# Weight conversion in blocks of 512 words, first-batch softmax by row sums, and a new split of small work between ScalarE and VectorE

## The chip, the cores and the metric

The kernel runs on one core of one Trainium2 chip. The metric is the device time of one execution in microseconds; the kernel before was timed three times, with a median of 1607.3 us (1606.66 to 1612.92).

## What is computed

Pooled attention followed by two MLPs, on 2304 tokens. Queries are averaged in pairs, so 4 batches of 8 heads have 576 queries against 1152 keys of width 64. The cut reference:

```python
q_pool = q.reshape(B, H, S // 2, 2, D).mean(axis=3)
scores = (1 / sqrt(D)) * q_pool @ k.transpose(0, 1, 3, 2)
attn = exp(scores - max(scores)); attn = attn / (sum(attn) + 1e-9)
x = (attn @ v), heads side by side          # 2304 x 512
h = x @ moe_w_in;  x = maximum(0.01 * h, h) @ moe_w_out       # 512 -> 2048 -> 512
h = x @ moe2_w_in; x = where(h > 0, h, exp(min(h, 0)) - 1) @ moe2_w_out
```

The weights of the MLPs arrive as 64-bit floats, that is as pairs of 32-bit words, and are converted on the chip.

## The kernel before

**Units of work.** Attention goes by pairs of heads, 16 pairs in all, four for each batch. For one head the 576 queries are two halves of 288, and the 1152 keys are nine blocks of 128. `weigh` multiplies one key block with one half (two matmuls into an `e` bank of PSUM), and ScalarE takes the exponential into `pt`. `value` multiplies `pt` with the value block and sums the nine blocks of a half in the single `o` bank. Before that, `maxima` finds each query's largest score: PE fills an `s` bank with 384 scores and VectorE (DVE) reduces it. The queries' part with the largest score in it (`ql`) is transposed into `qB`, so that the maximum is subtracted by the matmul itself.

**Batch 0 differs** (`FULL = (0,)`). It multiplies the unrounded exponentials in full precision, a matmul that shows as two instructions in the trace. Its value tile carries columns of ones beside the 64 value columns, so the sums of the exponentials come out in the other half of the `o` bank. At the end of each half ScalarE copies the sums to `tm` (L573), DVE takes their reciprocal over 64 x 288 (L575) and multiplies (L577). Only then is `o` free for the next half. Batches 1 to 3 instead sum the exponentials in `pacc` on DVE, and once a pair `normalise` turns these into quotients: ten small matmuls against ones (L599), three small DVE operations, transposes through the single `t` bank, and a multiplication on DVE.

**Queries.** `q_split` adds the two queries of a pair on POOL (L428), scales on DVE (L430), rounds on DVE into `qh` (L432), and leaves the rest `ql` to POOL (L435).

**Weights.** Each MLP has 32 tiles of 128 x 512, converted once and kept in DRAM in two parts. `convert` works in blocks of `CW` = 256: a load into `cr` (a ring of two), two DVE operations on the high word (L292, L295), two on ScalarE (L298 scales the low word, L300 takes the size of the high one into a tile `cm`), an addition on POOL (L302) and a last DVE operation (L304). Then the tile is rounded on ScalarE (L325), the rest formed on POOL (L327), and `ws` (a ring of three) is stored. `CONV` spreads the 32 tiles of the first MLP over the attention of batch 0, those of the second over most of batch 1.

**MLPs.** `mlp` splits its input into a rounded part `xs` (on DVE, L262) and a rest, then runs three matmuls for each product (L714 up, L752 down). The first MLP of batch 0 begins when the attention of batch 0 is done.

**Order.** Every operation goes into `Program` with an engine, a cost and a rank; `schedule` replays these costs and fixes one order for each engine. On the chip each engine runs its instructions in that order, so an instruction that waits holds up all those behind it on its engine. Transfers go through SP's queue in the same manner.

## Time and profile before

| | us |
|---|---|
| median of three runs | 1607.3 |
| profiled execution | 1605.11 |
| its span, first to last instruction | 1603.3 |
| PE busy | 1461.6 |
| DVE busy | 1072.8 |
| ScalarE (ACT) busy | 885.6 |
| POOL busy | 565.9 |

Busy time counts an engine's instructions, not its waits. Pairs of heads begin their first `weigh` at 28, 93, 148, 211 (batch 0), 270, 374, 485 and 561 us (batch 1), which gives the stretches that are used below; the later pairs follow at 82 to 93 us each. All numbers of "the span" are microseconds from the first instruction. A group of a line gives count, busy time, mean of one in ns, then the idle time of the engine just before and what ended it.

### The profile page before, as it was taken

To read this page: it belongs to the slowest core of one execution; us is meant where nothing else is said; L and a number is where in the kernel's file an instruction comes from. 1 tells how busy PE (TensorE), PEld (TensorE's weight loads), DVE (VectorE), ACT (ScalarE), POOL (GpSimd) and SP (SyncE) were. 2 spreads that over 40 slices of the span, in tenths; PEclk is the share of its full clock that TensorE was granted. 3 is DMA by queue.
4 is the path that set the end of the run, shared out by engine and by line. 5 is a ranking of instruction groups with operands and counts; after the bars stand their busy time and mean duration, and the time that the engine had idled before them with its cause. 6 is when DMAs were issued, how large, how long until landed. Compare 5 with 4: busy or idle time off the path is not lost.

```text
span 1603.3 us, 28154 instructions
## 1 busy us (share of the span) xinstructions
PE 1461.6 (91%) x9884; PEld 1379.9 (86%) x9884; DVE 1072.8 (67%) x2461; ACT 885.6 (55%) x2429; POOL 565.9 (35%) x660
## 2 busy tenths in 40 slices
PE   5777887878988999999999999999999999799998
PEld 3566666877877999999999999899999999799898
DVE  6788788988989877766667667866767564123222
ACT  4465656766756766556546665565556662222432
POOL 6455554655655222322313222222222112123221
PEclk9799878989999999999999999999999999899999
DMA  7565555676776334443434343333443333444352
GB/s 219 196 199 187 169 175 169 224 248 228 231 249 207 95 119 136 135 155 114 149 105 135 123 140 122 113 122 135 134 128 113 101 110 105 135 157 159 132 184 70
DMA packets 94413, 245.63 MB, mean 153 GB/s; under 512 B 10048, under 2 KB 28480, under 8 KB 94272
## 3 DMA queue, kind: packets, MB, share of 16 engines
q1 hardware_dynamic: 94272, 243.83, 46.0%
q8 instruction: 78, 1.28, 0.3%
q14 instruction: 63, 0.52, 0.1%
HBM read 196.08 MB, written 38.27 MB: 146 GB/s over the span
## 4 chain that ended last, share of the span: by engine, by line
PE 66%; DVE 17%; DMA 8%; ACT 4%; issue 3%; POOL 2%; SPq 0%; ACTq 0%; POOLq 0%; DVEq 0%
PE h L714 18%; PE h L752 17%; PE o L561 6%; PE s L481 4%; PE o L557 3%; PE e L522 3%; PE e L523 3%; DVE m L485 3%; DMA cr<-in_moe_w_out_dram 2%; DVE ws L295 2%; DVE tm L575 2%; PE t L399 2%; DMA cr<-in_moe_w_in_dram 2%; PE e L714 2%; DMA raw<-in_q_dram 2%
## 5 line engine op out<-in xcount | busy, mean ns | idle before, releaser
L752 PE MATMUL h<-g,wo 128*128 128x288 f32 x2544 | 449.2, 299 | 9.8 <-DVE t L735 5.9
L714 PE MATMUL h<-xs,wi 128*128 128x288 f32 x2520 | 429.8, 309 | 20.1 <-DVE t L727 11.2
L714 PEld LDWEIGHTS h<-xs,wi 128*128 128x128 f32 x2520 | 376.8, 197 | 28.6 <-DVE t L727 13.4
L266 POOL TENSOR_TENSOR g<-t,g 128x288 fp32r<-128x288 f32 x256 | 209.0, 827 | 530.1 <-ACT g L260 525.1
L752 PEld LDWEIGHTS h<-g,wo 128*128 128x128 f32 x2544 | 382.5, 190 | 13.1 <-DVE t L735 7.0
L538 ACT ACTIVATE pt<-e 128x288 fp32r<-128x288 f32 x432 | 173.7, 409 | 189.8 <-PE e L523 186.3
L542 DVE TENSOR_TENSOR pt<-e,pt 128x288 fp32r<-128x288 f32 x384 | 173.3, 451 | 96.7 <-ACT e L540 95.3
L485 DVE TENSOR_REDUCE m<-s 128x1 f32<-128x384 f32 x384 | 201.7, 548 | 16.8 <-PE s L481 15.8
L561 PE MATMUL o<-pt,vn 128*128 128x288 f32 x864 | 193.2, 306 | 8.2 <-DVE pt L542 5.4
L481 PE MATMUL s<-kA,qA 128*128 128x384 f32 x384 | 152.0, 416 | 30.2 <-DVE m L485 23.7
L545 DVE TENSOR_TENSOR pacc<-e,pacc 128x288 f32<-128x288 f32 x384 | 171.8, 447 | 0.3
L522 PE MATMUL e<-qA,kA 128*128 128x288 f32 x504 | 166.5, 332 | 4.9 <-DVE pacc L545 4.0
L561 PEld LDWEIGHTS o<-pt,vn 128*128 128x128 f32 x864 | 144.1, 194 | 13.5 <-DVE pt L542 8.8
L540 ACT ACTIVATE e<-e 128x288 f32<-128x288 f32 x384 | 154.6, 408 | 0.3
L523 PE MATMUL e<-qB,kb 65*128 65x288 f32 x504 | 152.5, 304 | 0.0
L260 ACT ACTIVATE g<-t 128x288 fp32r<-128x288 f32 x256 | 109.6, 443 | 47.3 <-DVE t L735 23.4
L557 PE MATMUL o<-pt,vn 128*128 128x288 f32 x288 | 114.6, 493 | 21.7 <-DVE xu L577 18.9
L302 POOL TENSOR_TENSOR ws<-ws,cr 128x256 uint32<-128x256 uint32 x128 | 97.1, 764 | 104.9 <-DVE ws L295 55.0
L481 PEld LDWEIGHTS s<-kA,qA 128*128 128x128 f32 x384 | 76.4, 204 | 53.3 <-DVE m L485 40.2
L522 PEld LDWEIGHTS e<-qA,kA 128*128 128x128 f32 x504 | 98.1, 195 | 14.5 <-DVE pacc L545 9.2
L765 DVE TENSOR_TENSOR acc<-h,acc 128x288 f32<-128x288 f32 x158 | 71.2, 452 | 53.8 <-PE h L752 52.8
L327 POOL TENSOR_TENSOR ws<-ws 128x512 fp32r<-128x512 f32 x64 | 84.0, 1312 | 60.4 <-ACT ws L325 60.0
(129 smaller groups left out, 2237.7 us busy)
## 6 DMA issues: line engine op xcount, KB each, us to landing
wi<-w SPq DMA_DIRECT2D x128, 512.0 KB, 3.3
wo<-w SPq DMA_DIRECT2D x128, 512.0 KB, 4.8
w<-ws SPq DMA_DIRECT2D x64, 512.0 KB, 3.0
cr<-in_moe_w_in_dram SPq DMA_DIRECT2D x64, 256.0 KB, 2.9
cr<-in_moe_w_out_dram SPq DMA_DIRECT2D x64, 256.0 KB, 3.0
raw<-in_k_dram SPq DMA_DIRECT2D x32, 288.0 KB, 3.7
raw<-in_v_dram SPq DMA_DIRECT2D x32, 288.0 KB, 3.2
kb<-kA SPq DMA_DIRECT2D x32, 288.0 KB, 3.8
```

The lines of the kernel that those rows point to most:

```text
L266: lambda: eng.tensor_tensor(out=lo(), in0=src(), in1=f32(hi()), op=ALU.subtract),
L481: PE.matmul(out=st[:, 0:384], lhsT=qa(), rhs=kA[:, 384 * c:384 * c + 384], start=(n == 0), stop=(n == len(terms) - 1))
L485: prog.add("DVE", dve(384), rank, lambda st=st, c=c: V.tensor_reduce(out=m[:, i, c:c + 1], in_=st[:, 0:384], axis=AX.X, op=ALU.max), w=[(m ...
L522: PE.matmul(out=st[:, 0:HB], lhsT=kA[:, ks], rhs=qA[:, cols], start=True, stop=False)
L523: PE.matmul(out=st[:, 0:HB], lhsT=kB[:, ks], rhs=qB[:, cols], start=False, stop=True)
L538: prog.add("ACT", act(HB), rank - LE, lambda: A.activation(out=pt[:, 0], in_=st[:, 0:HB], func=ACTF.Exp), w=[(pt, 0)], r=[st])
L542: prog.add("DVE", dve(HB), rank, lambda: V.tensor_tensor(out=pt[:, 1], in0=p(), in1=f32(pt[:, 0]), op=ALU.subtract), w=[(pt, 1)], r=[pw, ( ...
L545: prog.add("DVE", dve(HB), rank, lambda: V.tensor_tensor(out=acc[:, cols], in0=p(), in1=acc[:, cols], op=ALU.add), w=[(acc, hf)], r=[pw, ( ...
L557: PE.matmul(out=o[:, 0:HB], lhsT=f32(vn[:, c, :]), rhs=f32(pt[:, 0]), start=(c == 0), stop=(c == KC - 1))
L561: PE.matmul(out=o[:, 0:HB], lhsT=vn[:, c, :], rhs=pt[:, a, :], start=(c == 0 and a == 0), stop=(c == KC - 1 and a == 1))
L714: PE.matmul(out=h[:, 0:HB], lhsT=wi[:, a, c, :], rhs=xs[c][:, e, cols], start=(c == 0 and a == 0 and e == 0), stop=(c == DC - 1 and a == 1))
L752: PE.matmul(out=y[:, 0:HB], lhsT=w[f][1][:, a, d * 128:(d + 1) * 128], rhs=g[f][:, e, cols], start=(f % FC == 0 and a == 0 and e == 0), st ...
```

## The change

- **Sums by columns in batch 0.** At the end of a half ScalarE copies the 64 value rows of `o` into `xu` and one row of the sums into row 0 of a `pacc` tile. Reciprocal and multiplication of the half go; `normalise` now runs for batch 0 too, with matmuls of one row.
- **Scale in Exp.** The queries are no longer scaled; the exponentials take `scale=SCALE`.
- **Rounding of q** goes from DVE to ScalarE, and so does the rounded part of `xs` in both MLPs.
- **Conversion** in blocks of 512: half as many loads, DVE, ScalarE and POOL operations, each of twice the size. `cm` goes: the size of the high word is written over that word. `ws` has two buffers instead of three. `cr` still has two, of twice the size.
- **Banks of batch 0.** The four banks `e e h h` were used in turn for `weigh`; now `s s h h` are used in turn for `maxima`, and `weigh` has the two `e` banks.
- The planner's cost of `normalise`'s matmuls is doubled.

```diff
-    QSCALE = 0.5 / float(D) ** 0.5
+    SCALE = 0.5 / float(D) ** 0.5
-    CW = 256
+    CW = 512
-    WSB = 3
+    WSB = 2
-    EARLY = {'e': 'eehh'}
+    EARLY = {'s': 'sshh'}
...
-            mag = sb("cm", [128, CW], F32, CB)
...
-            prog.add("ACT", act(CW, sbuf=True), rank, lambda r=r, mag=mag: A.activation(
-                out=mag.ap, in_=r[:, :, 1].bitcast(F32), func=ACTF.Abs), w=[mag], r=[(r, 1)])
+            prog.add("ACT", act(CW, sbuf=True), rank, lambda r=r: A.activation(
+                out=r[:, :, 1].bitcast(F32), in_=r[:, :, 1].bitcast(F32), func=ACTF.Abs),
+                w=[(r, 1)], r=[(r, 1)])
...
-        prog.add("DVE", dve(n * D, True), rank, lambda: V.tensor_scalar(
-            out=qs(), in0=qs(), scalar1=QSCALE, scalar2=None, op0=ALU.mult), w=[src], r=[src])
-        prog.add("DVE", dve(2 * n * D, True), rank, lambda: V.tensor_copy(
+        prog.add("ACT", act(2 * n * D, sbuf=True), rank, lambda: A.activation(
             out=qh.ap.rearrange("p n (t d) -> p n t d", t=2),
-            in_=qs().unsqueeze(2).to_broadcast([128, n, 2, D])), w=[qh], r=[src])
+            in_=qs().unsqueeze(2).to_broadcast([128, n, 2, D]), func=ACTF.Copy), w=[qh], r=[src])
...
+        if b in FULL:
+            if hf == 0:
+                pacc[b, hp, j] = sb("pacc", [128, NQ], F32, 3)
+            sums = pacc[b, hp, j]
+            prog.add("ACT", act(HB), rank - LE, lambda: A.activation(
+                out=x[hi, cols], in_=o[hi, 0:HB], func=ACTF.Copy), w=[(x, (j, hf))], r=[o])
+            prog.add("ACT", act(HB), rank - LE, lambda: A.activation(
+                out=sums[0:1, cols], in_=o[lo.start:lo.start + 1, 0:HB], func=ACTF.Copy),
+                w=[(sums, hf)], r=[o])
+            return
         tm = sb("tm", [128, HB])
-        if b in FULL:
-            prog.add("ACT", act(HB), rank - LE, lambda: A.activation(
-                out=tm[hi, :], in_=o[lo, 0:HB], func=ACTF.Copy, bias=1e-9), w=[tm], r=[o])
-            prog.add("DVE", dve(HB), rank - LE, lambda: V.reciprocal(
-                out=tm[hi, :], in_=tm[hi, :]), w=[tm], r=[tm])
-            prog.add("DVE", dve(HB), rank - LE, lambda: V.tensor_tensor(
-                out=x[hi, cols], in0=o[hi, 0:HB], in1=tm[hi, :], op=ALU.mult), w=[(x, (j, hf))], r=[o, tm])
-            return
...
-        if b not in FULL:
-            event(at + 9 + PVLAG + 0.1, normalise, at + 9 + PVLAG + 0.1, b, hp, e)
+        event(at + 9 + PVLAG + 0.1, normalise, at + 9 + PVLAG + 0.1, b, hp, e)
...
-                psplit(at, "DVE", XL[c], lambda t=t, cols=cols: t[:, 0, cols],
+                psplit(at, "ACT", XL[c], lambda t=t, cols=cols: t[:, 0, cols],
```

**Where instructions stand.** At the end of a half in batch 0, DVE had before (the conversion's operations around the reciprocal, the rounding of q and the multiplication):

```order
L295 SCALAR_TENSOR_TENSOR ws<-cr,ws 128x256
L575 RECIPROCAL tm<-tm 64x288
L432 CAST qh<-raw 128x512
L577 TENSOR_TENSOR xu<-o,tm 64x288
L292 TENSOR_SCALAR ws<-cr 128x256
```

These three in the middle are gone from DVE. At such an end of a half ScalarE has now (L528 the exponentials, L430 the roundings of q, L297 and L299 the conversion's two operations, L573 and L575 the two copies out of `o`):

```order
L430 ACTIVATE qh<-raw 128x512
L528 ACTIVATE pt<-e 128x288
L430 ACTIVATE qxh<-qrem 128x128
L297 ACTIVATE cr<-cr 128x512
L528 ACTIVATE pt<-e 128x288
L573 ACTIVATE xu<-o 64x288
L575 ACTIVATE pacc<-o 1x288
L528 ACTIVATE pt<-e 128x288 x4
```

What freed `o` on DVE now stands on ScalarE, two rows one behind the other, between exponentials.

In batch 1, where the second MLP's weights are converted, DVE had before (L542 and L545 the rest and the sum of the exponentials):

```order
L292 TENSOR_SCALAR ws<-cr 128x256
L430 TENSOR_SCALAR raw<-raw 128x4x64
L295 SCALAR_TENSOR_TENSOR ws<-cr,ws 128x256
L292 TENSOR_SCALAR ws<-cr 128x256
L295 SCALAR_TENSOR_TENSOR ws<-cr,ws 128x256
L542 TENSOR_TENSOR pt<-e,pt 128x288
L304 SCALAR_TENSOR_TENSOR ws<-cm,ws 128x256
L545 TENSOR_TENSOR pacc<-e,pacc 128x288
L304 SCALAR_TENSOR_TENSOR ws<-cm,ws 128x256
```

and has now, in the same stage (L540 and L543 are the former L542 and L545, L727 the activation of the first MLP):

```order
L540 TENSOR_TENSOR pt<-pacc,pt 128x288
L304 SCALAR_TENSOR_TENSOR ws<-cr,ws 128x512
L291 TENSOR_SCALAR ws<-cr 128x512
L540 TENSOR_TENSOR pt<-e,pt 128x288
L294 SCALAR_TENSOR_TENSOR ws<-cr,ws 128x512
L543 TENSOR_TENSOR pacc<-e,pacc 128x288
L727 TENSOR_TENSOR t_3561<-h,t_3561 128x288
```

A tile takes three rows of the conversion instead of six, with more other work between them.

On PE, at the passage from the first pair to the second, there stood before (L557 the value matmul, L522 and L523 the two of `weigh`, L399 transposes):

```order
L557 MATMUL o<-pt,vn 128x288
L399 MATMUL t<-identr,ql 65x128 x4
L522 MATMUL e<-qA,kA 128x288
L523 MATMUL e<-qB,kb_83 128x288
...
L399 MATMUL t<-identr,qxl 65x128
L557 MATMUL o<-pt,vn 128x288 x2
```

and there stand now (L555 the value matmul, L520 and L521 those of `weigh`, L600, L616 and L623 the three steps of `normalise`):

```order
L555 MATMUL o<-pt,vn 128x288
L600 MATMUL t<-ones_73,pacc 128x2 x10
L555 MATMUL o<-pt,vn 128x288
L520 MATMUL e<-qA,kA 128x288
L521 MATMUL e<-qB,kb_83 128x288
L555 MATMUL o<-pt,vn 128x288
L616 MATMUL t<-ident,rb 128x128 x4
...
L623 MATMUL t<-ident,rb 128x128
```

Two units of `value` and one of `weigh` stand between the sums and the transposes that wait for DVE's quotients.

## Rows read from the trace of the kernel before

**Rows 1.** Stretches: busy time of each engine (instructions), PE clock, DMA share, GB/s.

```profile
0.00:270.00 270.00, 203.91 (x890) 157.21 (x890) 214.39 (x406) 154.62 (x408) 144.23 (x175) 0.85 0.59 190
270.00:374.00 104.00, 88.48 (x553) 79.79 (x551) 97.80 (x224) 75.62 (x210) 63.96 (x68) 0.93 0.67 227
374.00:485.00 111.00, 94.08 (x605) 86.74 (x605) 95.64 (x232) 72.10 (x202) 63.80 (x69) 0.92 0.71 232
485.00:561.00 76.00, 71.17 (x501) 67.82 (x500) 70.99 (x164) 51.50 (x146) 31.28 (x35) 0.98 0.47 150
561.00:1330.00 769.00, 752.73 (x5540) 742.87 (x5539) 522.93 (x1279) 448.85 (x1257) 199.10 (x234) 0.98 0.38 125
```

**Rows 2.** Chain of work that ended last, 28 to 270 us, shares by line.

```profile
by line: PE o L557 21.9%; DVE tm L575 11.0%; DVE m L485 9.9%; issue 6.4%; PE s L481 4.8%; DMA cr<-in_moe_w_in_dram 4.1%; DMA raw<-in_q_dram 4.1%; DVE ws L295 3.9%; PE t L399 3.6%; DVE ws L292 3.4%; DVE ws L304 3.1%; DMA cr<-in_moe_w_out_dra
```

**Rows 3.** The same chain, 270 to 485 us, shares by line.

```profile
by line: DMA cr<-in_moe_w_out_dram 13.6%; DVE ws L295 8.7%; DMA cr<-in_moe_w_in_dram 8.6%; DVE ws L304 6.8%; DVE pt L542 6.0%; issue 6.0%; DVE ws L292 5.9%; DVE m L485 5.8%; DVE pacc L545 5.0%; PE h L714 4.9%; DVE t L727 2.6%; POOL ws L302 
```

**Rows 4.** Chain in order of time, pieces: start us, length us, what.

```profile
215.79 1.95 DVE tm L575
...
218.22 0.47 DVE xu L577
...
218.74 1.63 PE o L557 x4
```

**Rows 5.** DVE's groups, 0 to 270 us.

```profile
L295 DVE SCALAR_TENSOR_TENSOR ws<-cr,ws 128x256 uint32<-128x256 uint32 x64 | 38.2, 598 | 1.2
L304 DVE SCALAR_TENSOR_TENSOR ws<-cm,ws 128x256 f32<-128x256 f32 x63 | 34.7, 555 | 20.8 <-POOL ws L302 19.7 <-ACT cm L300 1.1
L575 DVE RECIPROCAL tm<-tm 64x288 f32<-64x288 f32 x15 | 29.1, 1941 | 0.3 <-ACT tm L573 0.2
L292 DVE TENSOR_SCALAR ws<-cr 128x256 uint32<-128x256 uint32 x64 | 28.6, 449 | 13.6 <-DMA cr<-in_moe_w_in_dram 9.5 <-DMA cr<-in_moe_w_out_dram 4.0
L432 DVE CAST qh<-raw 128x512 fp32r<-128x512 f32 x11 | 9.4, 850 | 6.8 <-PE t L399 6.7
L430 DVE TENSOR_SCALAR raw<-raw 128x256 f32<-128x256 f32 x11 | 7.1, 645 | 2.0 <-POOL raw L428 2.0
```

**Rows 6.** The chain around 405 us, pieces in order of time.

```profile
402.59 0.74 POOL ws L302
...
403.35 4.42 DMA cr<-in_moe_w_in_dram
...
409.32 0.75 POOL ws L302
...
410.08 4.28 DMA cr<-in_moe_w_out_dram
```

**Rows 7.** Two DVE lines, all executions: least, median and longest ns.

```profile
L292 DVE TENSOR_SCALAR ws<-cr x128: 220/290/1517, 6.4 to 509.7; 128x256 uint32<-128x256 uint32 x128
L432 DVE CAST qh<-raw x32: 354/519/1608, 8.9 to 1192.0; 128x512 fp32r<-128x512 f32 x32
```

**Rows 8.** Groups of the whole span: prices at 512 columns, and ScalarE's rounding at 288.

```profile
L327 POOL TENSOR_TENSOR ws<-ws 128x512 fp32r<-128x512 f32 x64 | 84.0, 1312 | 60.4 <-ACT ws L325 60.0
L325 ACT ACTIVATE ws<-ws 128x512 fp32r<-128x512 f32 x64 | 40.4, 630 | 41.8 <-DVE ws L304 41.4 <-DMA cr<-in_moe_w_out_dram 0.3
L618 DVE TENSOR_TENSOR xu<-t,xu 128x512 f32<-128x512 f32 x12 | 8.3, 688 | 4.3 <-PE t L615 4.3
L260 ACT ACTIVATE g<-t 128x288 fp32r<-128x288 f32 x256 | 109.6, 443 | 47.3 <-DVE t L735 23.4 <-DVE t L727 22.4 <-PE h L752 0.3
```

**Rows 9.** Who waited for whom, 0 to 270 us: total us, times, longest.

```profile
PEld s L481 <- DVE m L485: 28.4, 42, 3.3
...
ACT ws L325 <- DVE ws L304: 21.9, 13, 6.5
```

**Rows 10.** Later in the chain: the sums of a `normalise` on PE.

```profile
564.10 2.13 PE t L599 x20
```

**Rows 11.** DMA issues of the whole span: the store of a converted tile, KB, median us to landing.

```profile
w<-ws SPq DMA_DIRECT2D x64, 512.0 KB, 3.0
```

More of the change, by code (lines that the diff above doesn't have):

```diff
@@ L299, in convert @@
                 out=r[:, :, 0], in_=r[:, :, 0], func=ACTF.Copy, scale=2.0 ** -29), w=[(r, 0)], r=[(r, 0)])
-            prog.add("ACT", act(CW, sbuf=True), rank, lambda r=r, mag=mag: A.activation(
-                out=mag.ap, in_=r[:, :, 1].bitcast(F32), func=ACTF.Abs), w=[mag], r=[(r, 1)])
+            prog.add("ACT", act(CW, sbuf=True), rank, lambda r=r: A.activation(
+                out=r[:, :, 1].bitcast(F32), in_=r[:, :, 1].bitcast(F32), func=ACTF.Abs),
+                w=[(r, 1)], r=[(r, 1)])
             prog.add("POOL", pool(CW), rank, lambda t=t, r=r: G.tensor_tensor(
                 out=t(), in0=t(), in1=r[:, :, 0], op=ALU.add), w=[(dst, n)], r=[(dst, n), (r, 0)])
-            prog.add("DVE", dve(CW), rank, lambda t=t, mag=mag: V.scalar_tensor_tensor(
-                out=t().bitcast(F32), in0=mag.ap, scalar=MIN_HI, in1=t().bitcast(F32),
-                op0=ALU.is_ge, op1=ALU.mult), w=[(dst, n)], r=[(dst, n), mag])
+            prog.add("DVE", dve(CW), rank, lambda t=t, r=r: V.scalar_tensor_tensor(
+                out=t().bitcast(F32), in0=r[:, :, 1].bitcast(F32), scalar=MIN_HI, in1=t().bitcast(F32),
+                op0=ALU.is_ge, op1=ALU.mult), w=[(dst, n)], r=[(dst, n), (r, 1)])
     kept = {}
@@ L530, in weigh @@
             prog.add("ACT", act(HB), rank - LE, lambda: A.activation(
-                out=f32(pt[:, 0]), in_=st[:, 0:HB], func=ACTF.Exp), w=[pt], r=[st])
+                out=f32(pt[:, 0]), in_=st[:, 0:HB], func=ACTF.Exp, scale=SCALE), w=[pt], r=[st])
             return
@@ L538, in weigh @@
         prog.add("ACT", act(HB), rank - LE, lambda: A.activation(
-            out=pt[:, 0], in_=st[:, 0:HB], func=ACTF.Exp), w=[(pt, 0)], r=[st])
+            out=pt[:, 0], in_=st[:, 0:HB], func=ACTF.Exp, scale=SCALE), w=[(pt, 0)], r=[st])
         prog.add("ACT", act(HB), rank - LE, lambda: A.activation(
-            out=p(), in_=st[:, 0:HB], func=ACTF.Exp), w=[pw], r=[st])
+            out=p(), in_=st[:, 0:HB], func=ACTF.Exp, scale=SCALE), w=[pw], r=[st])
         prog.add("DVE", dve(HB), rank, lambda: V.tensor_tensor(
@@ L598, in total @@
                 for j in range(2):
-                    PE.matmul(out=t[:, 0, 4 * w + 2 * j:4 * w + 2 * j + 2], lhsT=pacc[b, hp, j][:, at:at + 128],
-                              rhs=ones2, start=True, stop=True)
-        prog.add("PE", 10 * 111, rank, total, w=[t], r=[pacc[b, hp, j] for j in range(2)])
+                    row = slice(0, 1) if b in FULL else slice(0, 128)
+                    PE.matmul(out=t[:, 0, 4 * w + 2 * j:4 * w + 2 * j + 2], lhsT=pacc[b, hp, j][row, at:at + 128],
+                              rhs=ones2[row], start=True, stop=True)
+        prog.add("PE", 10 * 222, rank, total, w=[t], r=[pacc[b, hp, j] for j in range(2)])
         prog.add("DVE", 100, rank, lambda: V.tensor_scalar(
@@ L781, in store @@
             p = bank(tag, [128, 512], F32, bufs)
-            o = sb("cr", [128, DM], F32, CB)
+            o = sb("cr", [128, 2 * DM], F32, CB)
             def tr(p=p, t=t, n=n):
@@ L792, in store @@
             prog.add("ACT", act(DM), at, lambda p=p, o=o, n=n: A.activation(
-                out=o[0:n, :], in_=p[0:n, :], func=ACTF.Copy), w=[o], r=[p])
+                out=o[0:n, 0:DM], in_=p[0:n, :], func=ACTF.Copy), w=[o], r=[p])
             rows = out[b * NQ:(b + 1) * NQ]
@@ L797, in store @@
             prog.add("SP", 60, at, lambda o=o, n=n, rows=rows: nc.sync.dma_start(
-                out=rows, in_=o[0:n, :]), r=[o])
+                out=rows, in_=o[0:n, 0:DM]), r=[o])
     n9 = 2 * QT + 1
```

## The prediction

> **What bounds the kernel now.** I read the table of stretches first [rows 1]. From 561 us on PE is busy 752.73 of 769 us, 98%: nothing that other engines gain there is worth time. Before that it is different. In 0 to 270 us (attention of batch 0) PE is busy 203.91 us and DVE 214.39 us, at a mean clock of 0.85 of 2.4 GHz, that is with some of the time at the lower level of 1.2; in the two stretches to 485 us PE has 85% (88.48 of 104, 94.08 of 111) and DVE 94% and 86%. So 485 us hold all that can be won, and DVE is the longest engine in most of them.
>
> The chain of waits says what stands in the way. From 28 to 270 us [rows 2] PE's value matmul has 21.9%, but DVE's reciprocal 11.0%, its maxima 9.9%, and the three DVE operations of the conversion 3.9 + 3.4 + 3.1 = 10.4%. From 270 to 485 us [rows 3] the loads of raw weights have 13.6 + 8.6 = 22.2% (48 us of 215) and the conversion's DVE operations 21.4% (46 us). Why is seen in the chain around 405 us [rows 6]: POOL's addition ends at 403.33, the next load into the same buffer starts at 403.35 and takes 4.42 us, the addition of that block starts at 409.32, and the load after it at 410.08. The ring of two `cr` buffers is closed on itself: a buffer turns in 6.7 us here and holds half a tile, and engines that meet an unlanded block stop with all that stands behind it.
>
> **The change part by part.** The sums are against the profiled run, 1605.1 us (span 1603.3 and 1.8 around it); the median shown is 2.2 us above it.
>
> *End of a half in batch 0.* In the chain [rows 4] the reciprocal starts at 215.79 and takes 1.95 us, the multiplication ends at 218.69, and PE's value matmul follows at once. 15 reciprocals are 29.1 us of DVE [rows 5], and 11.0% of 242 us, 26.6 us, lie on the chain: nearly all. In their place ScalarE makes a second copy; no such copy of one row is in the trace, and its bounds are zero (hidden) and the price of a 288-column rounding, 0.443 us [rows 8]; I take the latter, 15 x 0.44 = 7 us. Net -20; bounds 0 (PE meets another wait at once) and -27.
>
> *Quotients of batch 0.* Three of the four new `normalise` calls fall into batch 0's attention. Each costs PE 2.13 us for the sums [rows 10]; that matmuls of one row take as long as those of 128 is assumed, with half of it as the lower bound. Its transposes wait for three DVE operations, a 512-column multiplication (0.688 us [rows 8]) follows, and the single `t` bank holds back the next head's transposes meanwhile. Two `value` units and one `weigh` cover part of it. I take 4 us a pair, +12; bounds +4 and +20. The fourth call, in batch 1, adds PE's 2.1 us to that stretch.
>
> *Conversion, DVE.* A block costs 598 + 555 + 449 ns [rows 5], a tile twice that, 3.2 us. At 512 columns nothing in the trace is the same operation: the nearest are 0.688 us for two operands [rows 8] and 0.354 to 0.519 us for one [rows 7], so 1.73 to 1.90 us free of conflicts. The present excess is large: L292 takes 290 ns in the median, 449 in the mean of batch 0 and up to 1517 [rows 7, 5], which is DVE standing still while POOL works. By L292, 0.16 us an instruction, a tile of three instructions would have 0.5 us of it, or 1.0 us if the doubled POOL instruction doubles each wait: 2.2 to 2.9 us a tile against 3.2, a gain of 0.3 to 1.0 us for each of some 60 tiles. The Trainium skill speaks against more here: "SBUF — State Buffer", section "SBUF: two separate sides", says that the port pair of DVE and GpSimd is locked for a whole instruction and the loser fully blocks, so longer POOL additions lengthen each wait; the trace agrees as far as the 1517 ns stand beside POOL operations of 1312 ns [rows 7, 8], and by the rule alone the upper price holds, a gain of 0.3 us a tile.
>
> *Conversion, rings.* A `cr` buffer now turns once a tile: a load (4.4 us as there, twice the bytes), 1.1 us for two DVE operations, POOL 1.31 us [rows 8], the last DVE operation 0.69 (it now reads `cr`, so it holds the buffer too), and hand-offs and queues, for which I take 2.0 us (410.08 - 403.35 - 4.42 - 0.75 leaves 1.6 us for two short DVE operations and all hand-offs now): 9.5 us, for two buffers 4.8 us a tile against 6.7 now. The ring of `ws` shrinks to two: the same 5.1 us of work and hand-offs without the load, ScalarE 0.63, POOL 1.31 [rows 8], the store 3.0 [rows 11], some 10 to 11 us with queues, 5 to 5.5 us a tile. 32 tiles then need 160 to 176 us, against 252 today (128 blocks from 6.4 to 509.7 us [rows 7], 7.9 us a tile), so PE should come next.
>
> *q and xs to ScalarE.* DVE loses 9.4 + 7.1 us in batch 0 [rows 5] and half of it in the next stretches. ScalarE gains about 0.63 us a head (as L325, [rows 8]) and 64 roundings of `xs` at 0.443, 28 us in all. It is busy 154.62 of 270 and 448.85 of 769 us [rows 1], so late in the run they are hidden; if that cover failed, the eight roundings ahead of each MLP would cost 3.5 us on ScalarE, less what DVE needs for them today. Path: -5 in batch 0 (0 to -10), 0 later (-5 to +5).
>
> *Banks.* PE's weight loads wait 28.4 us for the maxima on DVE [rows 9]; four banks and a freer DVE take part of it: -5 (0 to -12). `weigh` falls from four banks to two, so PE can be two units ahead of the exponentials instead of four: +3 (0 to +10).
>
> **Sum.** 0 to 270 us: -20 + 12 - 10 (conversion's DVE and load waits; 0 to -20) - 5 - 5 + 3 = -25, to about 245. 270 to 485 us: PE's work is 88.48 + 94.08 + 2 = 184.6 us, less some 4 us as its clock rises from 0.925 towards 0.98. Its share must lie between today's 85% and the 98% of rows 1; I take 93%, that of the stretch after (71.17 of 76), which is the nearest: 180.6 / 0.93 = 194, -21. 485 to 561 us: PE 71.17 at 96%, -2. Later 0. In all -48: 1557 for the profiled run, **1559** with the 2.2 us to the median.
>
> **Rivals.**
> *PE becomes the bound in both stretches.* Batch 0: DVE falls to about 155 us (214 - 29 - 17 - 20 for the conversion + 6 for the quotients), ScalarE stays near 160, and PE's 204 + 8 us shrink by perhaps 12 with the clock; at 90% with 10 us of start, 232, -38. Batch 1 at 98%: 184, -31. With -3 after: 1535. For it: no other engine would be above 80%. Against: in batch 0 four engines pass work in small steps, each in a fixed order.
> *The `ws` ring takes the place of the `cr` ring.* If stores land late or ScalarE and POOL queue, 15 us a turn are 7.5 us a tile, as now. Then batch 1 keeps its 215 us and the conversion's -10 is lost: -15, **1592**. For it: today's tile waits at every hand-off. Against: it needs 4 us more than I worked out.
> *Slower: ScalarE stops the exponentials.* The in-place size of the high word must now wait for DVE's second operation, and behind it on ScalarE stand exponentials. With two `e` banks PE runs dry when ScalarE stops for longer than about 0.8 us (one `weigh` and `value`). A stop of s us at each of 64 tiles costs (s - 0.8) x 64; it eats my 48 us at s = 1.55, and at 2.0 gives 1607 - 48 + 77 = 1636. Against: ScalarE's like wait for DVE's last operation comes to 21.9 us in batch 0, 0.7 us for each of 31 tiles [rows 9].
> *Nothing moves*: gains of DVE meet waits for loads everywhere, 1605.
>
> **How the numbers follow.** Forecast (1540 to 1582) 0.56; PE-bound (1520 to 1540) 0.17; `ws` ring (1582 to 1600) 0.15; slower 0.07; no change 0.05. Within 0.5%, 8 us and about what a measurement of this kernel can tell from no change, lies the no-change case and a part of the `ws` ring, 0.08. Range 1525 to 1597, which leaves out some 0.2.
>
> **What would show it.** Right: the second batch starts near 245 instead of 270 us, the pair that starts at 561 us near 513; loads of raw weights fall to under 8% of the chain in batch 1; no DVE wait for `tm`; DVE under 165 us in the first stretch. Wrong: DVE's first conversion operation waiting for the store of `ws`; PE waiting for exponentials in batch 0 for more than 20 us; ScalarE's idle time in front of the size of the high word above 1 us a tile; or PE idle around the quotients' transposes for more than 4 us a pair.

## The result, and the profile after

The changed kernel takes **1567.4 us** (median of four runs, 1566.65 to 1572.01) against 1607.2 (1606.66 to 1612.92): a ratio of 0.9751, 95% interval 0.9721 to 0.978. Forecast were 1559 us and a gain of 48 us; the gain is 40. Engines in the profiled run: PE busy 1450.3 us (1461.6 before), DVE 939.9 (1072.8), ScalarE 917.0 (885.6), span 1564.9 (1603.3), mean granted clock 0.959 (0.951).

The stretches of the kernel after, cut where the same pairs start as in [rows 1] (columns as there):

```profile
0.00:247.00 247.00, 199.24 (x982) 159.16 (x982) 140.11 (x258) 161.37 (x385) 142.40 (x143) 0.90 0.65 211
247.00:346.00 99.00, 85.49 (x523) 78.38 (x523) 85.61 (x169) 72.64 (x182) 59.85 (x54) 0.88 0.67 219
346.00:455.00 109.00, 93.90 (x615) 87.57 (x614) 87.06 (x182) 71.08 (x173) 63.26 (x55) 0.94 0.72 237
455.00:537.00 82.00, 75.42 (x524) 72.47 (x525) 64.32 (x142) 56.05 (x156) 31.84 (x33) 0.96 0.42 142
537.00:1306.00 769.00, 759.35 (x5628) 752.00 (x5626) 502.19 (x1216) 470.65 (x1319) 201.78 (x236) 0.98 0.39 129
```

DVE fell from 214.39 to 140.11 us in batch 0, but PE's share in batch 1 hardly rose: 86% in both stretches against 85% before. The last row, of the same length as that of before, holds 6.6 us more of PE's work in it.

For all kernels below the run is cut at the starts of three pairs: A ends where batch 1 starts (pair 4), B is pairs 4 and 5, "6" is pair 6, C is all from the start of pair 7. These four are spans of one profiled run each, in us; medians and ratios are of all runs, each against runs of the kernel before on the same chip. The profiled run of conv_only lies 7 us above its median and that of no_conv 8 us, so their stages add up to more than the median; the others lie within 4 us.

| kernel | median | ratio (95%) | A | B | 6 | C |
|---|---|---|---|---|---|---|
| before | 1607.2 | | 270.2 | 214.9 | 76.3 | 1041.9 |
| forecast | 1559 | | 245 | 194 | 74 | as before |
| after | 1567.4 | 0.9751 (0.9721–0.978) | 247.6 | 207.8 | 81.8 | 1027.5 |
| quot_only | 1594.0 | 0.9913 (0.989–0.9936) | 246.9 | 223.4 | 71.2 | 1048.8 |
| conv_only | 1603.8 | 0.9975 (0.9955–0.9994) | 267.4 | 219.5 | 76.9 | 1045.4 |
| xs_only | 1595.6 | 0.9907 (0.9877–0.9938) | 271.1 | 217.0 | 72.3 | 1032.9 |
| no_conv | 1559.5 | 0.9673 (0.9641–0.9704) | 240.4 | 218.3 | 75.0 | 1031.7 |
| xs_dve | 1577.7 | 0.9823 (0.9784–0.9861) | 249.3 | 213.2 | 76.6 | 1037.9 |
| banks_back | 1583.8 | 0.9839 (0.9812–0.9866) | 269.3 | 201.5 | 82.3 | 1029.9 |
| cost111 | 1580.5 | 0.981 (0.9767–0.9854) | 243.4 | 230.6 | 79.3 | 1023.7 |
| ws3 | 1563.4 | 0.9723 (0.9698–0.9748) | 253.1 | 197.7 | 80.2 | 1032.6 |
| rings | 1568.2 | 0.9744 (0.9715–0.9773) | 265.1 | 188.2 | 84.2 | 1029.7 |
| lat45 | 1524.1 | 0.9461 (0.9432–0.949) | 222.0 | 204.5 | 74.6 | 1017.3 |
| ws3_lat45 | 1515.5 | 0.9404 (0.938–0.9428) | 225.2 | 187.3 | 77.6 | 1020.7 |
| before_lat45 | 1575.6 | 0.9786 (0.9758–0.9814) | 253.5 | 186.9 | 97.7 | 1036.3 |

So the gain of the change, as the two profiled runs show it, lies elsewhere than forecast: 22.6 us in A (25 forecast), 1.6 in B and pair 6 together (23 forecast), 14.4 in C (0 forecast).

The chain of waits of the kernel after, shares by line, first for 27 to 247 us, then for 247 to 455 us, as [rows 2, 3] are for before ("issue" is time in which the engine waited for nothing that the profile shows):

```profile
by line: DMA w<-ws 16.2%; issue 11.7%; PE o L555 8.4%; POOL ws L327 5.6%; POOL ws L302 4.6%; DVE ws L304 4.5%; DVE m L483 3.8%; PE t L600 3.4%; DMA qrem<-in_q_dram 3.1%; PE e L520 2.9%; DMA cr<-in_moe_w_out_dram 2.9%; DVE ws L294 2.6%; PE e
by line: DMA w<-ws 19.1%; DMA cr<-in_moe_w_out_dram 7.8%; issue 7.8%; DVE ws L304 5.2%; DVE ws L294 4.9%; PE h L714 4.5%; POOL ws L327 3.9%; DMA cr<-in_moe_w_in_dram 3.9%; DVE ws L291 3.8%; DVE pt L540 3.4%; POOL ws L302 3.0%; PE h L752 2.4
```

The reciprocal of a half (`DVE tm`) is gone, the maxima fell from 9.9% to 3.8%, and the loads of raw weights in batch 1 from 22.2% to 7.8 + 3.9 = 11.7%. What leads in both is new: the **store of a converted tile**, 36 us and 40 us. "issue" rose from 6.4% to 11.7% in batch 0; where that time comes from was not traced. How it gets onto the chain, in pieces in order of time (start, length, what):

```profile
387.33 1.29 POOL ws L327
...
388.63 6.43 DMA w<-ws
...
395.09 0.44 DVE ws L291
```

POOL finishes a tile, its store takes 6.43 us, and only then does DVE start the tile after next in the same buffer. All that stands behind this instruction on DVE waits as well.

The waits for conversion transfers in the kernel after, 0 to 455 us (who waited for whom: total us, times, longest):

```profile
DVE ws L291 <- DMA w<-ws: 50.2, 21, 7.5
...
ACT cr L297 <- DMA cr<-in_moe_w_out_dram: 24.7, 14, 4.2
...
ACT cr L297 <- DMA cr<-in_moe_w_in_dram: 23.2, 16, 5.3
...
DVE ws L291 <- DMA cr<-in_moe_w_in_dram: 7.0, 1, 7.0
```

They sum to 105.1 us. In the kernel before, the same waits, 0 to 485 us, are these, 65.5 us in all and none for a store:

```profile
ACT cr L298 <- DMA cr<-in_moe_w_in_dram: 20.3, 16, 4.5
...
DVE ws L292 <- DMA cr<-in_moe_w_in_dram: 15.4, 12, 3.8
DVE ws L292 <- DMA cr<-in_moe_w_out_dram: 15.3, 12, 4.1
...
ACT cr L298 <- DMA cr<-in_moe_w_out_dram: 14.5, 14, 4.0
```

### The profile page after: what moved, and what is told of

The parts are those of the page before. It is cut to its first block, busy times and chain, and to the rows that moved or that the text cites. A ratio compares the mean times of both kernels' runs of the same rounds, so it can differ in the third digit from the quotient of the medians.

```text
span 1564.9 us, 27712 instructions
## 1 busy us (share of the span) xinstructions
PE 1450.3 (93%) x9984; PEld 1381.9 (88%) x9984; DVE 939.9 (60%) x2097; ACT 917.0 (59%) x2429; POOL 561.1 (36%) x596
## 4 chain that ended last, share of the span: by engine, by line
PE 66%; DMA 12%; DVE 8%; ACT 5%; POOL 4%; issue 4%; SPq 0%; DVEq 0%; ACTq 0%; POOLq 0%
PE h L752 18%; PE h L714 18%; PE o L559 6%; DMA w<-ws 5%; PE s L479 3%; PE e L520 3%; PE e L521 3%; DMA cr<-in_moe_w_out_dram 2%; PE e L752 2%; PE s L714 2%; PE t L600 2%; PE e L714 2%; PE s L752 2%; PE t L399 2%; DVE ws L304 1%
## 5 line engine op out<-in xcount | busy, mean ns | idle before, releaser
L266 POOL TENSOR_TENSOR g<-t,g 128x288 fp32r<-128x288 f32 x256 | 209.9, 830 | 515.4 <-ACT g L260 507.2
L540 DVE TENSOR_TENSOR pt<-e,pt 128x288 fp32r<-128x288 f32 x384 | 173.5, 452 | 104.0 <-ACT e L538 102.5
L520 PE MATMUL e<-qA,kA 128*128 128x288 f32 x576 | 199.5, 348 | 10.9 <-DVE pacc L543 5.4
L559 PE MATMUL o<-pt,vn 128*128 128x288 f32 x864 | 195.4, 308 | 12.3 <-DVE pt L540 10.7
L483 DVE TENSOR_REDUCE m<-s 128x1 f32<-128x384 f32 x336 | 175.8, 548 | 16.1 <-PE s L479 14.7
L521 PE MATMUL e<-qB,kb 65*128 65x288 f32 x576 | 176.4, 307 | 0.0
L543 DVE TENSOR_TENSOR pacc<-e,pacc 128x288 f32<-128x288 f32 x384 | 171.7, 447 | 0.4
L520 PEld LDWEIGHTS e<-qA,kA 128*128 128x128 f32 x576 | 113.9, 198 | 23.6 <-DVE pacc L543 9.5
L260 ACT ACTIVATE g<-t 128x288 fp32r<-128x288 f32 x256 | 110.2, 444 | 28.3 <-DVE t L727 13.9
L479 PE MATMUL s<-kA,qA 128*128 128x384 f32 x336 | 116.2, 370 | 3.5 <-DVE m L483 2.6
L521 PEld LDWEIGHTS e<-qB,kb 65*128 65x128 f32 x576 | 114.2, 198 | 4.2 <-ACT qB L505 0.3
L266 POOL TENSOR_TENSOR vn<-raw,vn 128x576 fp32r<-128x576 f32 x24 | 34.9, 1453 | 214.6 <-ACT vn L260 168.0
L302 POOL TENSOR_TENSOR ws<-ws,cr 128x512 uint32<-128x512 uint32 x64 | 87.1, 1363 | 60.8 <-DVE ws L294 48.8
L555 PE MATMUL o<-pt,vn 128*128 128x288 f32 x288 | 103.4, 444 | 5.0 <-POOL vn L466 2.8
```

What stands on the lines that cost most here:

```text
L266: lambda: eng.tensor_tensor(out=lo(), in0=src(), in1=f32(hi()), op=ALU.subtract),
L479: PE.matmul(out=st[:, 0:384], lhsT=qa(), rhs=kA[:, 384 * c:384 * c + 384], start=(n == 0), stop=(n == len(terms) - 1))
L483: prog.add("DVE", dve(384), rank, lambda st=st, c=c: V.tensor_reduce(out=m[:, i, c:c + 1], in_=st[:, 0:384], axis=AX.X, op=ALU.max), w=[(m ...
L520: PE.matmul(out=st[:, 0:HB], lhsT=kA[:, ks], rhs=qA[:, cols], start=True, stop=False)
L521: PE.matmul(out=st[:, 0:HB], lhsT=kB[:, ks], rhs=qB[:, cols], start=False, stop=True)
L540: prog.add("DVE", dve(HB), rank, lambda: V.tensor_tensor(out=pt[:, 1], in0=p(), in1=f32(pt[:, 0]), op=ALU.subtract), w=[(pt, 1)], r=[pw, ( ...
```

## The experiments

Theory at the start: batch 0's gain comes from the quotients and the lighter DVE, and batch 1 stood still because the ring of two `ws` buffers had taken the place of the ring of `cr`. Rivals: the conversion costs time by its form and not by its buffers; the gains are those of the fixed order of instructions; what was gained late is noise. The twelve runs follow in the order of the questions. None of them leaves out part of the computation.

### One part alone, in the kernel before

**The quotients alone.** The branch for batch 0 from the diff above, `normalise` for all batches with its planner's cost; all else as before.

```diff
-            prog.add("DVE", dve(HB), rank - LE, lambda: V.reciprocal(
-                out=tm[hi, :], in_=tm[hi, :]), w=[tm], r=[tm])
...
+            prog.add("ACT", act(HB), rank - LE, lambda: A.activation(
+                out=sums[0:1, cols], in_=o[lo.start:lo.start + 1, 0:HB], func=ACTF.Copy),
+                w=[(sums, hf)], r=[o])
...
-        if b not in FULL:
-            event(at + 9 + PVLAG + 0.1, normalise, at + 9 + PVLAG + 0.1, b, hp, e)
+        event(at + 9 + PVLAG + 0.1, normalise, at + 9 + PVLAG + 0.1, b, hp, e)
```

> The kernel before with one part alone: batch 0's quotients by row sums and normalise, with two copies on ScalarE. Theory, from the prediction: the freed o bank gives 20 us in the first 270 us, the four calls of normalise take back 12 to 14, so 1597 to 1602, pair 4 starting near 262. Rival: the reciprocals on DVE were most of what held batch 0, and the calls of normalise are hidden: 1585 to 1590.

Measured: 1594.0 us, A 246.9. This part alone brings all of what the change brings in A. Its stretch row, 0 to 247 us:

```profile
0.00:247.00 247.00, 197.46 (x944) 153.79 (x944) 184.86 (x383) 155.93 (x418) 142.35 (x171) 0.91 0.63 205
```

DVE is busy 184.86 us here and 140.11 in the kernel after, in the same 247 us. In the kernel after, the 45 us by which DVE is busy less than here shortened batch 0 by nothing. The time lies between the two ranges expected. B and C are 8.5 and 6.9 us longer than before and pair 6 is 5.1 shorter, so that nearly half of the gain is given back; why was not found out.

**The conversion alone.**

```diff
-    CW = 256
+    CW = 512
-    WSB = 3
+    WSB = 2
...
-                out=mag.ap, in_=r[:, :, 1].bitcast(F32), func=ACTF.Abs), w=[mag], r=[(r, 1)])
+                out=r[:, :, 1].bitcast(F32), in_=r[:, :, 1].bitcast(F32), func=ACTF.Abs),
+                w=[(r, 1)], r=[(r, 1)])
```

> The kernel before with the conversion alone changed: blocks of 512, size of the high word in place, two ws buffers. Theory: the cr ring gives way to the ws ring, DVE gains some 0.6 us a tile but waits for stores; 1595 to 1605, with DVE waiting 30 us or more for stores of ws. Rival: the larger blocks are the main gain of the whole change: 1580 to 1590.

Measured: 1603.8 us over ten runs, ratio 0.9975 (0.9955 to 0.9994); A 267.4, B 219.5. Half as many instructions on three engines, with one `ws` buffer less, are worth 0.25%. DVE's waits for stores are there, but they come to 20.3 us up to 487 us and not to 30.

**The roundings of `xs` alone.**

```diff
-                psplit(at, "DVE", XL[c], lambda t=t, cols=cols: t[:, 0, cols],
+                psplit(at, "ACT", XL[c], lambda t=t, cols=cols: t[:, 0, cols],
```

> The kernel before with the rounded part of xs on ScalarE and nothing else. Theory: this move alone carries what the changed kernel gains after 537 us, since at each passage between MLPs PE waits for roundings and rests that DVE made one behind the other: 1593 to 1600, with the stretches of pairs 8 and 12 each 3 to 4 us shorter. Rival: it takes the lighter ScalarE or DVE of the whole change; then 1603 to 1610.

Measured: 1595.6 us, 0.9907 (0.9877 to 0.9938): 14 us, of which 9.0 are in C. The traces show where. The chain of the kernel before ahead of a second MLP (pieces: start, length, what):

```profile
666.57 0.95 DVE xs L262 x2
...
674.07 0.85 DVE xs L266
...
676.27 0.40 PE e L522
...
676.80 1.26 PE h L752 x9
```

The same passage in the kernel after:

```profile
641.79 0.67 ACT xs L260 x2
...
643.19 1.32 DVE xs L266 x2
...
645.59 0.44 PE s L479
...
646.50 3.00 PE h L752 x21
```

Before, DVE made roundings (L262) and rests (L266) one behind the other, 10.2 us from the first rounding to the matmuls at 676.80. After, ScalarE makes the roundings (L260), DVE follows with the rests, and from 641.79 it is 4.7 us. The passage itself gains less than these two numbers suggest, since other work of ScalarE now stands ahead of its roundings: the chain is away from PE for 9.7 us before (666.57 to 676.27) and for 7.8 us after (637.79 to 645.59). Such passages lie in pairs 8 and 12. In xs_only these two take 89.8 and 90.9 us instead of 93.3 and 93.4, which is 6.0 of the 9.0 us in C; the other 3 us were not located.

### One part undone, in the kernel after

**`xs` back on DVE** (the line above, the other way round).

> The changed kernel with the rounded part of xs back on DVE, all else as changed. Theory: the 13.7 us that the changed kernel gains after 537 us come from this move, at the passages from one MLP to the next, where DVE made roundings and rests one behind the other; then the time is 1578 to 1583 and the gain after pair 7 is gone. Rival: they come from DVE's lighter load as a whole (q off DVE); then 1565 to 1570.

Measured: 1577.7 us, 10 more than after, and C is longer by as much: 1037.9 against 1027.5. The run before and this one agree: the roundings of `xs`, with the order that comes with them, are worth 10 to 14 us.

**The conversion of before** (blocks of 256, `cm`, three `ws`), all else as after.

```diff
-    CW = 512
+    CW = 256
-    WSB = 2
+    WSB = 3
...
+            mag = sb("cm", [128, CW], F32, CB)
```

> The changed kernel with the conversion as before (blocks of 256, a tile of its own for the size of the high word, three ws buffers); quotients, q, xs and banks stay changed. Theory: the conversion's blocks bring nothing in batch 0 and a little in batch 1, as when they were changed alone: 1565 to 1575, batch 0 ending at 242 to 250 us. Rival 1: within the whole change they cost time in batch 0, since DVE waits for stores of ws there: 1550 to 1560. Rival 2: they carry part of the gain: 1580 or more.

Measured: 1559.5 us, 0.9673 (0.9641 to 0.9704), an interval wholly under that of after. In this company the new conversion is a loss of about 8 us. Where it loses them isn't shown: in the profiled run A is 7.2 us shorter without it (240.4), B 10.5 longer, pair 6 6.8 shorter and C 4.2 longer, but this run took 1567.2 us, as long as the kernel after. Stores of `ws` take 2.9 us here in batch 0 instead of 4.6, and DVE waits for none.

**The banks of before.**

```diff
-    EARLY = {'s': 'sshh'}
+    EARLY = {'e': 'eehh'}
```

> The changed kernel with the four banks given back to weigh, and two for maxima. Theory from the prediction: the exchange is worth 2 us in batch 0, so 1565 to 1571. Rival 1: two banks for weigh cost more than four for maxima give, PE waits for exponentials: 1555 to 1562. Rival 2: the four banks of maxima carry the gain of batch 0: 1575 to 1585.

Measured: 1583.8 us; A 269.3, as in the kernel before. Two waits of this kernel, 0 to 265 us:

```profile
DVE ws L291 <- DMA w<-ws: 52.2, 16, 9.5
...
PEld s L479 <- DVE m L483: 29.2, 43, 2.8
```

The second of these in the kernel after, 0 to 247 us:

```profile
PEld s L479 <- DVE m L483: 4.1, 16, 0.8
```

The kernel after uses `h` banks for `maxima` as well; there the same wait adds 3.6 us.

PE waits for the maxima as it did before ([rows 9], 28.4 us), and DVE, on which the maxima stand, waits 52.2 us for stores against 34.5 in the kernel after up to 247 us. But quot_only has the old banks too and A of 246.9: it has the old conversion, without waits for stores. So the exchange of banks is worth 22 us in A where DVE stops for stores. Where it doesn't, A can be nearly as short with the old banks: 246.9 in quot_only against 240.4 in no_conv, which has the new banks and the new split of q besides. That the stops for stores are why the banks matter is argued from these rows; the old banks in no_conv or in the better order below were not tried.

**The planner's cost of `normalise`** back to the old number; the instructions are the same, their order isn't.

```diff
-        prog.add("PE", 10 * 222, rank, total, w=[t], r=[pacc[b, hp, j] for j in range(2)])
+        prog.add("PE", 10 * 111, rank, total, w=[t], r=[pacc[b, hp, j] for j in range(2)])
```

> The changed kernel with the planner's cost of the sums in normalise as before. It changes only the order. Theory: the sums take 2.13 us on PE, as the doubled cost says, so the old cost lets PE's order run ahead of the chip; the difference is small, 1564 to 1574. Rival: the doubled cost moves later work of PE for the worse (the kernel with the quotients alone lost 7 us after pair 7); then 1555 to 1562.

Measured: 1580.5 us, with runs from 1570 to 1586; A 4 us shorter, B 23 us longer. Neither range was met. An edit that only reorders moves this kernel by some 13 us. Every difference of that size between the kernels here may hold a part that is only order.

### Buffers, or order?

**Three `ws` buffers.** Room for it comes from sharing one identity matrix.

```diff
-    WSB = 2
+    WSB = 3
...
-    ident = const.tile([128, 128], F32, name="ident")
...
+    ident = identr[:, :].bitcast(F32)
```

> The changed kernel with three ws buffers instead of two (the unrounded identity matrix shares its place with the rounded one, so that the third buffer finds room; nothing else differs). Theory: in batch 1 the ring of ws took the place of the ring of cr; DVE's first conversion operation waited 50 us in all for stores of ws, and DMA w<-ws has 16 to 19% of the chain from 27 to 455 us. With a third buffer these waits fall below 10 us, the stretch from pair 4 to pair 7 (now 247 to 537 us) shrinks by 12 to 25 us, and the time goes from 1567 to about 1545 to 1555. Rival: PE's in-order waits for DVE and ScalarE set the pace there, the store waits are only where the engine happens to stand; then the waits move to loads of cr or to POOL and the time stays at 1562 to 1572.

Measured: 1563.4 us, within the intervals the same as after. B is 10 us shorter, A 5.5 longer. The waits for conversion transfers, 0 to 455 us (line numbers are one higher here):

```profile
DVE ws L292 <- DMA cr<-in_moe_w_in_dram: 40.6, 19, 5.3
DVE ws L292 <- DMA cr<-in_moe_w_out_dram: 34.7, 14, 6.1
ACT cr L298 <- DMA cr<-in_moe_w_in_dram: 28.2, 15, 3.7
...
DVE ws L292 <- DMA w<-ws: 15.8, 6, 4.6
...
ACT cr L298 <- DMA cr<-in_moe_w_out_dram: 15.0, 12, 3.0
```

The wait for the store falls from 50.2 to 15.8 us, and the waits for loads rise from 54.9 to 118.5. The interval (0.9698 to 0.9748) overlaps with that of no_conv, which has three buffers too, so how much of no_conv's 8 us belongs to the buffer and how much to the form of the conversion isn't separated.

**Three of both.** `cr` gets a third buffer too, for which one of six `wo` buffers goes.

```diff
-    CB = 2
+    CB = 3
-    WOB = 6
-    WSB = 2
+    WOB = 5
+    WSB = 3
```

> The changed kernel with three buffers for ws and three for cr (room from one wo buffer less and from the shared identity matrix). Theory: in batch 0 and 1 the conversion's rings set the pace, first that of ws, with a third ws buffer that of cr; with both wider DVE's waits for loads and stores fall below 15 us in the first 460 us, batch 0 ends near 235 us and the time is 1540 to 1552. Rival: the pace is set by the order in which PE, ScalarE and DVE meet, and rings only take up what is left over: 1560 to 1568.

Measured: 1568.2 us. B falls to 188.2, A is 265.1. And the wait for the store is still there with three buffers, here 0 to 455 us:

```profile
DVE ws L292 <- DMA w<-ws: 61.4, 19, 10.9
```

So the theory falls in this form. A third buffer takes the waits from the store to the loads, and a third of both (with one `wo` buffer less, whose part wasn't separated) takes them back to the store; A is longer both times. The planner uses each buffer to place the conversion earlier, and DVE still meets transfers that haven't landed. That last step is argued from these rows, and the next run puts it to the test.

**The order alone.** New theory: the planner counts 2500 ns for any transfer and its hand-off, while 512 KB need more than that here. The transfers of the kernel after, 27 to 247 us (KB each, median us from issue to landing):

```profile
w<-ws SPq DMA_DIRECT2D x30, 512.0 KB, 4.6
cr<-in_moe_w_in_dram SPq DMA_DIRECT2D x15, 512.0 KB, 3.8
cr<-in_moe_w_out_dram SPq DMA_DIRECT2D x15, 512.0 KB, 4.3
```

So it places instructions of DVE and ScalarE ahead of their data, and in a fixed order they hold up all behind them. One number of the planner is changed; no instruction is added or taken away and no buffer changes.

```diff
-    LATENCY = {"PE": 200, "SP": 2500, "DVE": 130, "DVE POOL": 200, "ACT": 155, "ACT POOL": 170, "POOL": 150,
+    LATENCY = {"PE": 200, "SP": 4500, "DVE": 130, "DVE POOL": 200, "ACT": 155, "ACT POOL": 170, "POOL": 150,
```

> The changed kernel with the planner's latency of a transfer at 4500 instead of 2500 ns; nothing but the order of instructions changes. In batch 0 of the changed kernel a converted tile takes 4.6 us to store and a raw one 3.8 to 4.3 us to load, so the planner places the operations that wait for them too early, and DVE and ScalarE stand still in front of them. Theory: with the truer number other work goes ahead of them, DVE's waits for stores and loads in the first 460 us fall from 57 to below 30 us and the time to 1545 to 1558. Rival: the rings themselves are too short, so that the work only stands elsewhere: 1562 to 1572.

Measured: **1524.1 us**, 43 less than after, A 222.0. The waits for the same transfers, 0 to 455 us:

```profile
DVE ws L291 <- DMA w<-ws: 28.3, 16, 6.6
...
ACT cr L297 <- DMA cr<-in_moe_w_out_dram: 7.4, 4, 2.3
...
DVE ws L291 <- DMA cr<-in_moe_w_in_dram: 6.0, 1, 6.0
ACT cr L297 <- DMA cr<-in_moe_w_in_dram: 4.4, 1, 4.4
```

They fell from 105.1 to 46.1 us. Both ranges expected were missed: the time is 21 us below the theory's, while DVE's own part of the waits fell from 57.2 us to 34.3 (28.3 and 6.0) and not below 30. The chain of 27 to 222 us, by line:

```profile
by line: PE o L555 17.9%; DVE m L483 11.6%; issue 6.3%; DMA w<-ws 5.7%; PE e L520 5.3%; PE e L521 4.8%; DVE ws L294 4.6%; PE t L600 4.1%; DVE ws L291 4.0%; POOL ws L302 3.4%; PE s L479 3.3%; PE t L399 3.1%; DVE mx L483 2.8%; ACT pt L528 2.7
```

The store fell from 16.2% to 5.7%, and PE's value matmul leads again. A is even below the 232 us of the rival in which PE bounds batch 0. The stretch row, to compare with the first of the kernel after:

```profile
0.00:222.00 222.00, 187.91 (x982) 153.22 (x983) 140.63 (x249) 156.93 (x376) 133.11 (x137) 0.93 0.66 220
```

PE is busy 11.3 us less with the same number of instructions, at a mean granted clock of 0.93 instead of 0.90. So of the 25 us between the two stretches 11.3 are PE's busy time and 13.7 its idle time.

**Both, and the order in the kernel before.**

> As lat45, with three ws buffers (room from the shared identity matrix). Theory: the ring and the placement are two parts of one wait; together 1535 to 1552. Rival: as for lat45 and for the third buffer alone, 1558 to 1566.

> The kernel before with the planner's latency of a transfer at 4500 instead of 2500 ns and nothing else, which tells what of the last two results belongs to the change and what to the order. Theory: before, the first 270 us are also held by the reciprocals on the o bank and by DVE's load, which the order cannot hide, so the truer number gives less than the 43 us that it gave the changed kernel: 1580 to 1600, batch 0 ending at 255 to 265 us; the change is then worth more than its 40 us, 55 to 75. Rival: the misplaced waits were the whole loss of both kernels: 1560 to 1570, and the change is worth its 40 us as before.

Measured: 1515.5 us for both, the fastest of all, 5.96% (5.72 to 6.2) under the kernel before and below both ranges; with the better order the third `ws` buffer is worth 9 us, and 17 in B. The kernel before gains 34 us by the same number (1575.6 us), its waits for conversion transfers falling from 65.5 to 27.8 us. So the mis-set number isn't the change's doing. But it costs the changed kernel more: with it at 4500 the change is worth 1575.6 - 1524.1 = 51 us instead of 40, of which A has 31.5, B and pair 6 together 5.5 and C 19.0. The 1575.6 lie between what the two theories expected, and neither was met: the number costs the kernel before 34 us and the kernel after 43, a difference that is smaller than the 13 us of cost111. For the same reason it isn't shown that the whole 43 us come from shorter waits, though three kernels gain by the same number. Whether the new conversion is still a loss in this order was not tried.

## Why the prediction was right or wrong

The sign, the time within 8.4 us and the main range (1540 to 1582) held, for reasons that were half right. That the number came so close is in part luck, since two errors of opposite sign nearly cancel: batch 1 gave 21 us less than forecast (B and pair 6 together) and the late run 14 us more.

- **End of a half, and quotients of batch 0: right in kind, too small.** Forecast were -20 and +12; alone they give -23. PE's wait for the multiplication, in the kernel before from 0 to 270 us and its counterpart in the kernel after from 0 to 247 us, is what was to go, and it went:

```profile
PE o L557 <- DVE xu L577: 18.9, 10, 3.2
PE o L555 <- ACT pacc L575: 1.8, 6, 0.5
```

  Which of the two terms was mis-sized isn't separated. The 80 matmuls of one row up to 262 us keep PE busy for 13.5 us, 3.4 us a pair at the clock of that stretch, above the 2.13 that were assumed. But the steps around them are hidden: PE's sums wait 1.3 us in all, its transposes not at all. `PE t L600` is 3.4% of the chain, 7.5 us for three pairs; in quot_only the same sums have 5.3% of the chain from 29 to 247 us, 11.6 us, close to the 12. What brought the rest of the 23 us is open; 29 us of reciprocals less on DVE is the likely place, which was not tested. PE's lines, 0 to 262 us (busy us, mean ns, idle before):

```profile
L600 PE MATMUL t<-ones,pacc 1*128 1x2 f32 x80 | 13.5, 296 | 1.3 <-ACT qB L505 1.3
L616 PE MATMUL t<-ident,rb 128*128 128x128 f32 x12 | 3.1, 412 | 0.0
```

- **ScalarE's copies: price right, but mostly hidden.** The one-row copy takes 401 ns, against a taken price of 443. PE waits 1.8 us for it in all (above), not the 7 us that were put on the path. Groups of ScalarE, 0 to 247 us:

```profile
L573 ACT ACTIVATE xu<-o 64x288 f32<-64x288 f32 x15 | 6.0, 403 | 0.6 <-PE o L555 0.4
...
L575 ACT ACTIVATE pacc<-o 1x288 f32<-1x288 f32 x15 | 6.0, 401 | 0.2
```

- **Conversion on DVE: price right, worth nothing.** DVE's groups, 0 to 247 us:

```profile
L304 DVE SCALAR_TENSOR_TENSOR ws<-cr,ws 128x512 f32<-128x512 f32 x32 | 30.6, 967 | 31.5 <-POOL ws L302 27.0 <-ACT cr L299 4.5
L294 DVE SCALAR_TENSOR_TENSOR ws<-cr,ws 128x512 uint32<-128x512 uint32 x33 | 27.6, 844 | 0.7
L291 DVE TENSOR_SCALAR ws<-cr 128x512 uint32<-128x512 uint32 x33 | 15.0, 454 | 49.9 <-DMA w<-ws 34.5 <-DMA cr<-in_moe_w_in_dram 7.0 <-POOL kn L266 6.3
```

  A tile costs 0.97 + 0.84 + 0.45 = 2.27 us; 2.2 to 2.9 were forecast. The excess over the medians 427, 692 and 693 is 0.45 us a tile, 0.15 an instruction, as before. In batch 1 it is larger, 247 to 455 us:

```profile
L304 DVE SCALAR_TENSOR_TENSOR ws<-cr,ws 128x512 f32<-128x512 f32 x28 | 28.1, 1003 | 5.6 <-POOL ws L302 3.1 <-ACT cr L299 2.2
L294 DVE SCALAR_TENSOR_TENSOR ws<-cr,ws 128x512 uint32<-128x512 uint32 x27 | 24.1, 892 | 0.3
L291 DVE TENSOR_SCALAR ws<-cr 128x512 uint32<-128x512 uint32 x27 | 17.1, 634 | 15.7 <-DMA w<-ws 15.7
```

  A tile costs 2.53 us there, with an excess of 0.24 us an instruction, against 0.15 in the kernel before (270 to 485 us); conv_only has 0.23 in batch 0. So beside POOL's longer operations the wait grew in these two stretches, and in batch 0 of this kernel it didn't. "SBUF — State Buffer" of the Trainium skill, section "SBUF: two separate sides", says that the loser of the shared port pair fully blocks; the prediction took it as a warning that each wait would grow with POOL's instruction, which leaves a gain of 0.3 us a tile. The traces agree with the blocking: no execution of these three operations that overlapped no instruction of POOL took more than 0.43 us (blocks of 256) or 0.70 us (512), and all longer ones, up to 1.5 and 1.9 us, overlapped one. The size was less than feared: the gain is 0.9 us a tile in batch 0 and 0.6 in batch 1, where a tile cost 3.14 us before, so the upper price was too high. But these 30 us of DVE for 32 tiles didn't shorten batch 0: conv_only gains 2.8 us in A, quot_only has the same A without it, no_conv a shorter one.

- **Conversion, rings: the step that failed.** 5 to 5.5 us a tile were forecast; the 64 tiles take from 9.7 to 477.6 us, 7.4 us each, against 7.9 before. The pace alone says little, since the planner spreads the tiles over the pairs by rank: lat45 converts at 7.1 us a tile (8.6 to 458.9 us) and yet ends 43 us earlier. All executions of DVE's first operation (least, median, longest ns; first and last start), as in [rows 7]:

```profile
L291 DVE TENSOR_SCALAR ws<-cr x64: 411/427/1430, 9.7 to 477.6; 128x512 uint32<-128x512 uint32 x64
```

  Two terms of it were off. The store was put at 3.0 us [rows 11] and takes 4.6; and "hand-offs and queues" held no time in which DVE and ScalarE stand in front of a transfer that hasn't landed, of which the rows above show 105.1 us (65.5 before). This is the rival "the `ws` ring takes the place of the `cr` ring", with chance 0.15, and in batch 1 it came true as written: the store leads the chain and B + 6 keep 289.6 of 291.2 us. Its time, 1592, did not come, since A and C were shorter. And its cause was put too narrowly: ws3 and rings show that the depth of the rings alone isn't what holds it, and lat45 that the same rings run 43 us faster in another order.

- **Batch 1's sum: the number that failed.** PE's work in the two stretches is 179.4 us (85.49 + 93.90), close to the 180.6 of the sum, although the clock did not rise as assumed (0.88 and 0.94). But PE's share was taken at 93%; it is 86%. Between 85% and 98% the ends were both in the text, and the value near the lower end was right. The choice went by the stretch nearest in time, which has only some eight of the 128 conversion blocks in it, and not by the stretch itself.

- **q and xs to ScalarE: wrong late in the run.** The text said that PE at 98% left nothing to win there. Yet 2% of 769 us are 16 us, and PE's idle time in them fell to 9.7 us, its share rising from 97.9% to 98.7%. That is less than the 10 to 14 us of the two runs on `xs`: over all of C PE is also busy 7.6 us less than before (1003.6 and 996.0 us). DVE stood on the path at the passages of pairs 8 and 12. The part of q was never run alone, so -5 for batch 0 stays open.

- **Banks: wrong in size.** -5 and +3 were forecast; undoing it costs 16 us, 22 of them in A. That batch 0 as a whole came out right is thus a sum of terms that don't add: quotients alone 23, with all the rest but the banks 1, with the banks 23 again.

- **The slower rival** did not come: ScalarE's wait between DVE's second operation and the size of the high word is 0.38 us a tile, far under 1.55, and PE waits 5.2 us for exponentials. The waits in 0 to 247 us:

```profile
PE e L520 <- ACT pt L528: 5.2, 6, 1.8
...
ACT cr L299 <- DVE ws L294: 12.4, 12, 2.1
```

Of the signs named, these came true: the start of batch 1 (247.6), DVE under 165 us, no `tm` wait, and PE not idle around the quotients' transposes. These did not: the pair at 513 us (537) and the loads under 8% (11.7%). One sign against the forecast appeared: DVE's first operation waits for the store. Not explained is pair 6, 5.5 us longer than before.

## What to carry to other kernels

Where a planner fixes the order of work, its latency for a transfer is a tuning parameter like any other: compare it with the median from issue to landing in the trace, again after each change of transfer size, since an instruction placed ahead of its data stops its whole engine. Halving an engine's instructions bought next to nothing here, where the chain runs through other hand-offs; look which wait comes next, and price it by the share that the stretch itself has now. A stretch in which PE is busy for 98% can still give something, here 7 of its 16 idle microseconds, in part at passages where one engine does two steps in series and another can do the first. And when a forecast comes true, compare its terms with the stages: here two of them were off by 21 and 14 us in opposite directions.
